# A piece held back at the chunk borders, the last sums on VectorE, and the first x copied earlier

## The chip, the cores and the metric

The kernel runs on one core of a Trainium2 chip. The core has five engines that run side by side, each through its own list of instructions: TensorE (PE in the profile, with its weight loads as PEld), VectorE (DVE), ScalarE (ACT), GpSimd (POOL) and SyncE (SP, which here only issues DMAs). The metric is the device time of one execution in microseconds (us), as the median of several runs.

## The reference

All arithmetic is float32. Attention comes first: 8 batches of 8 heads, 576 positions, 64 values a head, and in each row of scores only the 32 largest survive. The result is laid out as 4608 tokens of 512 values, and a two-layer MLP with an exact gelu follows.

```python
scores = scale * np.matmul(q, k.transpose(0, 1, 3, 2))          # (8, 8, 576, 576)
kth = np.partition(scores, -32, axis=-1)[..., -32:-31]
scores = np.where(scores >= kth, scores, -1e9)
attn = np.exp(scores - scores.max(-1, keepdims=True))
attn = attn / (attn.sum(-1, keepdims=True) + 1e-09)
x = np.matmul(attn, v).transpose(0, 2, 1, 3).reshape(4608, 512)
h = x @ w_in                                                    # 4608 x 2048
out = (0.5 * h * (1.0 + erf(h / sqrt(2)))) @ w_out              # 4608 x 512
```

## The kernel before

**Items and steps.** The attention is cut into 144 items. An item is a pair of heads and a tile of 128 queries (the last 64 queries of two pairs share an item). The main loop (L1034) makes one step `n` per item and works on several items at once. In step `n` TensorE makes the scores of items ahead (`scores`, L358; even steps make two), the product of item `n - 3` with v (`attend`, L596; only every second item has one, since two query tiles are multiplied together), and the transposes of the attention weights of item `n - 2` (`transposes`, L513). ScalarE evicts the scores, does the softmax of item `n - 1` in two halves (`softmax`, L490), copies transposed weights (L537, L560, L574) and copies the product into `xT` (L620). VectorE searches the 32nd largest score of item `n` (`top_k`, L423). GpSimd normalises the weights of item `n - 1` (`normalise`, L507), and in its list this stands behind two small operations that wait for the threshold VectorE has found (`threshold`, L470).

**Chunks and MLP pieces.** The MLP works on chunks of 256 tokens (one in five has 128). A chunk can begin when all four head pairs of its tokens have been multiplied with v. Its work is cut into pieces of a few matmuls, and the pieces stand in one fixed list, `pieces` (L956): blocks of the first layer (`l1_piece`, L664, matmuls on L673) alternate with blocks of the second layer of an earlier unit (L755, L773 and L776, or `products`, L792, with matmuls on L809 and L811). Most chunks use a scheme of seven products for a 2 by 2 block product, so that sums of the gelus are needed first (`sums`, L698, four additions on GpSimd, L704 to L707).

`mlp(n)` (L959) issues the next `n` pieces unless the next one needs tokens that are not there (`pieces[done[0]][0] > ready[0]`) or the step's allowance `left[0]` is used up. The loop calls it in many places, so that TensorE has MLP work between attention work. `room_in(n)` (L973) gives about one block per step, and the first-layer block of a new 256-token chunk begins in just the step that makes the last product of its tokens. Such a step is called a chunk border here; from step 18 on there are 15, all with even numbers.

**Around the border.** After the product the loop asks for `copy_x` and for a piece, but at a border the next piece needs the tokens that have only just been multiplied. L1062 catches this case: the eight transposes of the next item are issued directly behind the product (`turned`), then the tails' transposes, and `ready` is set to the new tokens.

```python
product = attend(n - 3)
...
copy_x()
...
mlp(1)
...
turned = tr.pop() if few[0] and tr else None
if product and n > START and done[0] < len(pieces) and pieces[done[0]][0] > ready[0]:
    if turned:
        turned()
```

**The ends.** `START` is 10: step 10 completes the first chunk. In the steps up to it a softmax half is issued on ScalarE (L1052) ahead of the copy of the product. Behind the last step, only MLP pieces are left; the last unit pair has the number `NU - 2`, and `last_parts` (L882) makes and stores the last 256 rows' sums on VectorE.

PSUM tiles are shared by tag. The transposes and half of the scores use `pr`; the first layer and the other half of the scores use `l1`; the product, the tails and the seventh product use `z`. Each has one buffer, so that a writer waits until the earlier content has been evicted.

Of the kernel before, what the change touches and what calls it, by code (L numbers as in the profile page):

```python
# [14 lines left out]
def kernel(  # L15
# [19 lines left out]
    nc = tc.nc  # L35
# [289 lines left out]
    def pair_tile(name, tag="pr"):  # L325
        return ps.tile([P, 2, 512], f32, tag=tag, bufs=1, name=name)
# [186 lines left out]
    def transposes(i):  # L513

        if i < 0 or i >= N:
            return []
        t, s = items[i][1], S_of.pop(i)
        pr = [None]

        def tails(ahead):  # L520
            tp = bank("tp_t")
            keys = last_keys(ahead, tp) if ahead is not None and ahead < N else None
            at = P
            if t % 2 == 0:
                pt_now[0] = work.tile([P, 2 * NM + 1, 2 * P], f32, tag="pt", bufs=1, name="pt")
            if t < NM:
                nc.tensor.transpose(tp[:, at : at + P], s[:, SM : S + TL], ident)  # L527
            else:
                for r in range(2):
                    nc.tensor.transpose(  # L530
                        tp[0:TL, at + r * P : at + (r + 1) * P],
                        s[:, r * S + SM : (r + 1) * S], ident,
                    )
            if keys:
                keys()
            if t < NM:
                nc.scalar.copy(  # L537
                    out=pt_now[0][:, 2 * NM, t % 2 * P : (t % 2 + 1) * P], in_=tp[:, at : at + P]
                )
                return  # L540
            for e in range(2):
                c = slice(e * TL, (e + 1) * TL)
                nc.scalar.copy(
                    out=halves(pt_end[c, 0, :], e, P),
                    in_=halves(tp[0:TL, at : at + 2 * P], e, P),
                )

        x = t % 2 * P if t < NM else 0

        def turn_over(tp, e):  # L550
            first = e * (S + TL if t < NM else S)
            for j in range(NM):
                nc.tensor.transpose(  # L553
                    tp[:, j * P : (j + 1) * P], s[:, first + j * P : first + (j + 1) * P], ident
                )

        def main(e):
            tp = bank("tp")
            turn_over(tp, e)
            nc.scalar.copy(  # L560
                out=pt_now[0][:, e * NM : (e + 1) * NM, x : x + P],
                in_=tp.rearrange("p (j n) -> p j n", j=NM),
            )

        def turn_both():
            pr[0] = tp = pair_tile("tp")
            for e in range(2):
                turn_over(tp[:, e], e)

        def both():  # L570
            if pr[0] is None:
                turn_both()
            tp = pr[0]
            nc.scalar.copy(  # L574
                out=pt_now[0][:, 0 : 2 * NM, x : x + P],
                in_=tp.rearrange("p e (j n) -> p (e j) n", j=NM),
            )

        if few[0]:
            return [tails, lambda _: both(), turn_both]  # L580
        return [tails] + [lambda _, e=e: main(e) for e in range(2)]

    def copy_x():
        while copies:
# [113 lines left out]
    def sums(u):  # L698

        g = g_of[u].rearrange("p x (f n) -> p x f n", f=2)  # L700
        a11, a21, a12, a22 = (g[:, :, f, h * P : (h + 1) * P] for f in range(2) for h in range(2))
        t = work.tile([P, 2, 3, P], f32, tag="sum", bufs=1, name="sum")
        s1, s2, s4 = (t[:, :, x] for x in range(3))
        nc.gpsimd.tensor_tensor(s1, a21, a22, op=ALU.add)  # L704
        nc.gpsimd.tensor_tensor(s2, s1, a11, op=ALU.subtract)
        nc.gpsimd.tensor_tensor(a21, a11, a21, op=ALU.subtract)
        nc.gpsimd.tensor_tensor(s4, a12, s2, op=ALU.subtract)  # L707
        sums_of[u] = t

    def weight_sums(j):  # L710
# [171 lines left out]
    def last_parts(tok, k, a):  # L882

        dve, add = nc.vector.tensor_tensor, ALU.add
        if k == 0:
            end_of["y"] = y0, y1 = y_tile(), y_tile()
            nc.scalar.copy(out=y0[:, B1], in_=a[:, 0])
            end_of["a"] = a
            return
        y0, y1 = end_of["y"]  # L890
        s7 = y7[0]
        if k == 1:
            dve(y0[:, B2], a[:, 0], y0[:, B1], op=add)
            dve(y0[:, B1], end_of["a"][:, 1], y0[:, B1], op=add)
            nc.sync.dma_start(out=out[last_row : last_row + P, B1], in_=y0[:, B1])
            dve(s7, s7, y0[:, B2], op=add)
            dve(y1[:, B2], a[:, 1], s7, op=add)
            nc.sync.dma_start(out=out[last_row + P : last_row + 2 * P, B2], in_=y1[:, B2])
            dve(y0[:, B2], a[:, 1], y0[:, B2], op=add)
            return  # L900
        dve(y0[:, B2], a[:, 1], y0[:, B2], op=add)
        nc.sync.dma_start(out=out[last_row : last_row + P, B2], in_=y0[:, B2])
        dve(y1[:, B1], s7, a[:, 0], op=ALU.subtract)
        nc.scalar.dma_start(out=out[last_row + P : last_row + 2 * P, B1], in_=y1[:, B1])
# [129 lines left out]
    for n in range(ahead):  # L1034

        left[0] = room_in(n)
        few[0] = n > START + 2
        eager[0] = n > N
        if not waits(unit_in(n)):
            weights_add(unit_in(n))  # L1040
        larger(n + 1)
        for piece in squares_in.pop(n, []):
            piece()
        two = few[0] and n % 2 == 0 and n + 3 < N and items[n + 3][1] < NM
        scores(n + 2, two)
        if two:
            scores(n + 3)
        product = attend(n - 3)
        late = n > START
        if n <= START:  # L1050

            softmax(n - 1, 0)  # L1052
        copy_x()
        if waits(unit_in(n)):
            weights_size(unit_in(n))
            weights_add(unit_in(n))
        mlp(1)
        if few[0] and n % 2:
            run_gelus()
        tr = transposes(n - 2)  # L1060
        turned = tr.pop() if few[0] and tr else None
        if product and n > START and done[0] < len(pieces) and pieces[done[0]][0] > ready[0]:  # L1062

            if turned:
                turned()
            for piece in tr[:1]:
                piece(n + 2 if few[0] else None)
            tr, ready[0] = tr[1:], n_tok[0]
        if not few[0] and n > START:
            softmax(n - 1, 0)  # L1070
        mlp(1)
        if not late:
            softmax(n - 1, 1)
        if few[0]:
            softmax(n - 1, 0)
            if n % 2:
                mlp(ODD)
        mlp(1)
        if n < START:

            keep_busy((4 if product or n == 0 else 14) * (1 if n < 5 else 2), ident)
        prep = prep_in.pop(n, [])
        if n == START + 1:

            for piece in prep:
                piece(None)
            prep = []
        if len(prep) > 1 and len(tr) == 3:
            tr, prep = tr[:1] + prep[:1] + tr[1:], prep[1:]
        now = tr[:-1]  # L1090
        if few[0]:
            now, tr, prep = tr + prep[:1], [], prep[1:]
        for x, piece in enumerate(now):
            piece(n + 2 if few[0] else None)
            if n < START and product and x == 0:
                keep_busy(5 if n < 5 else 10, ident)
            ready[0] = n_tok[0]
            if few[0] and x == 2:
                break
            mlp(1)  # L1100
        ready[0] = n_tok[0]
        if late:
            softmax(n - 1, 1)
        smaller(n + 1)
        add_small(n - 1)
        for piece in tr[-1:] + prep:
            piece(None)
            mlp(1)
        if n == 1:
            keep_busy(8, ident)  # L1110

        run_gelus()
        mlp(left[0])
        run_gelus()
        if n < N:
            top_k(n, lambda: inverse(n - 1))
        else:
# [54 lines left out]
```

## Time and profile before

| what | before |
|---|---|
| median of 3 runs | 1548.0 us (1547.71 to 1549.83) |
| the profiled execution | 1547.88 us |
| its span, first to last instruction | 1546.1 us |
| mean granted TensorE clock | 0.996 |
| TensorE busy | 1513.3 us, 98% |
| VectorE busy | 1336.4 us, 86% |
| ScalarE busy | 1160.4 us, 75% |
| GpSimd busy | 1142.8 us, 74% |
| TensorE, weight loads | 1193.3 us, 77% |

The profile is one execution, recorded by the hardware. An instruction's row has its start and its length in microseconds, its engine, its line in the kernel, its operation, the tile written and the tiles read, and, in brackets, how long the engine was idle before it and which instruction ended that idle time. Matmuls are pipelined and overlap, and their ends are modelled. In the list of waits a row reads: engine, what waited, what it waited for, the total, how many times, and the longest. A product of float32 matrices shows as two TensorE instructions for each matmul of the code, a transpose as one.

### The profile page before, as it was taken

The numbers are of one execution on the slowest core, as the hardware profiler recorded it, in microseconds if no ns is written. First come the engines' busy times: TensorE is split into PE (matmuls) and PEld (weight loads), VectorE is DVE, ScalarE is ACT, GpSimd is POOL, SyncE is SP. The second block draws the span as 40 slices with busy tenths as digits, with TensorE's granted clock in tenths as the row PEclk, the third lists the DMA queues.
The fourth block names the chain that finished last, engine by engine and source line by source line (L and its number), as shares of the span: only waits on it lengthen the run. The fifth ranks groups of instructions, "written<-read, shape, count | busy, mean of one in ns | idle before, by whom it ended". The sixth has DMA issues, their size and how long they took to land. (4 is left out here: it accounts for less than half of the span.)

```text
span 1546.1 us, 28114 instructions
## 1 busy us (share of the span) xinstructions
PE 1513.3 (98%) x9240; PEld 1193.3 (77%) x9240; DVE 1336.4 (86%) x4583; ACT 1160.4 (75%) x2038; POOL 1142.8 (74%) x1291
## 2 busy tenths in 40 slices
PE   7899999999999999999999999999999999999998
PEld 5676577877777777888777778788778777788887
DVE  8999999989989988899989998988998998888700
ACT  6999987777777777777777777777777777787720
POOL 4896657777787868767787877776788787877732
PEclk9999999999999999999999999999999999999999
DMA  6424310012101110012201111011110111000000
GB/s 161 149 99 113 86 46 1 18 35 39 24 15 31 38 35 19 1 30 46 40 14 20 27 32 45 1 25 36 32 24 22 24 30 32 15 1 15 8 14 14
DMA packets 195027, 56.36 MB, mean 36 GB/s; under 512 B 185888, under 2 KB 186432, under 8 KB 194880
## 3 DMA queue, kind: packets, MB, share of 16 engines
q1 hardware_dynamic: 193616, 54.14, 14.9%
q8 instruction: 73, 1.20, 0.3%
q14 instruction: 74, 0.61, 0.1%
q10 hardware_dynamic: 1200, 0.39, 0.1%
q0 software_dynamic: 64, 0.03, 0.0%
HBM read 45.08 MB, written 9.44 MB: 35 GB/s over the span
## 5 line engine op out<-in xcount | busy, mean ns | idle before, releaser
L673 PE MATMUL h_ps<-xT,w_in_sb 128*128 128x256 f32 (+1 forms) x2560 | 539.6, 361 | 1.8 <-ACT xT L620 1.7
L673 PEld LDWEIGHTS h_ps<-xT,w_in_sb 128*128 128x128 f32 x2560 | 434.9, 191 | 73.5 <-issue 25.3
L450 DVE MAX8 top<-lists 128x8 f32<-128x288 f32 x792 | 321.4, 448 | 0.0
L507 POOL TENSOR_TENSOR s<-s,rden 128x1152 f32<-128x1152 f32 x144 | 302.9, 2104 | 0.3 <-DVE rden L482 0.3
L496 ACT ACTIVATE s<-s,bias 128x576 f32<-128x576 f32 x288 | 223.3, 775 | 11.9
L453 DVE MATCH_REPLACE8 lists<-top,lists 128x288 f32<-128x288 f32 x528 | 229.9, 443 | 0.0
L495 ACT ACTIVATE s<-s,neg 128x576 f32<-128x576 f32 x288 | 225.7, 784 | 2.9 <-POOL neg L475 2.8
L450 DVE MAX8 low<-lists 128x8 f32<-128x288 f32 x528 | 213.2, 446 | 0.0
L574 ACT COPY pt<-tp 128x1024 f32<-128x1024 f32 x133 | 134.9, 1014 | 95.9 <-PE tp L553 95.9
L488 POOL TENSOR_SCALAR den<-den 128x2 f32<-128x2 f32 x144 | 31.6, 219 | 224.6 <-ACT s L496 220.9
L421 POOL TENSOR_TENSOR lists<-lists 128x576 int32<-128x576 int32 x132 | 186.3, 1412 | 4.0
L413 POOL TENSOR_TENSOR lists<-s 128x576 int32<-128x576 int32 x132 | 185.9, 1408 | 0.0
L553 PE MATMUL tp<-ident,s 128*128 128x128 f32 x1152 | 150.4, 273 | 8.2 <-POOL s L507 8.2
L553 PEld LDWEIGHTS tp<-ident,s 128*128 128x128 f32 x1152 | 133.5, 141 | 27.9 <-POOL s L507 14.5
L615 PE MATMUL o<-pt,raw_v 128*64 128x256 f32 x1280 | 153.7, 385 | 0.4 <-ACT pt L560 0.4
L615 PEld LDWEIGHTS o<-pt,raw_v 128*64 128x64 f32 x1280 | 87.3, 137 | 86.1 <-issue 45.7
L475 POOL TENSOR_SCALAR neg<-kth 128x2 f32<-128x2 f32 x132 | 85.9, 651 | 90.6 <-DVE kth L466 90.0
L811 PE MATMUL y_ps<-w_out_sb,sum 128*128 128x256 f32 x480 | 142.8, 379 | 0.0
L378 ACT ACTIVATE s<-s_ps 128x1024 f32<-128x1024 f32 x127 | 124.2, 1025 | 15.1 <-PE s_ps L370 15.0
L370 PE MATMUL s_ps<-kt,qm 64*128 64x512 f32 x512 | 131.2, 626 | 0.8 <-ACT s L376 0.8
L482 DVE RECIPROCAL rden<-den 128x2 f32<-128x2 f32 x144 | 23.4, 162 | 124.0 <-POOL den L488 122.3
L453 DVE MATCH_REPLACE8 lists<-low,lists 128x288 f32<-128x288 f32 x264 | 115.0, 444 | 0.0
(148 smaller groups left out, 2771.3 us busy)
## 6 DMA issues: line engine op xcount, KB each, us to landing
raw_v<-in_v_dram SPq DMA_DIRECT2D x64, 128.0 KB, 2.3
out_dram<-y SPq DMA_DIRECT2D x30, 256.0 KB, 2.1
raw_q<-in_q_dram SPq DMA_DIRECT2D x112, 64.0 KB, 2.0
raw_k<-in_k_dram SPq DMA_DIRECT2D x112, 64.0 KB, 2.0
w_out_sb<-in_moe_w_in_dram SPq DMA_DIRECT2D x14, 511.8 KB, 4.7
w_out_sb<-in_moe_w_out_dram SPq DMA_DIRECT2D x10, 511.8 KB, 4.3
w_sum<-in_moe_w_out_dram SPq DMA_DIRECT2D x6, 511.8 KB, 4.2
raw_q<-in_q_dram SPq DMA_DIRECT2D x112, 8.0 KB, 1.8
```

The source lines that it names most:

```text
L413: nc.gpsimd.tensor_tensor(t[:, 1].bitcast(i32), a.bitcast(i32), b.bitcast(i32), op=ALU.add)
L421: nc.gpsimd.tensor_tensor(both, both, top, op=ALU.subtract)
L450: nc.vector.max(x[:, e], src[:, e])
L453: nc.vector.match_replace(dst[:, e], x[:, e], src[:, e], LOWEST)
L495: nc.scalar.activation(s, s, func=AF.Prelu, bias=st["neg"][:, e : e + 1], scale=1.0, alpha=STEEP)
L496: nc.scalar.activation(s, s, func=AF.Exp, bias=st["bias"][:, e : e + 1], scale=1.0, accum_out=st["den"][:, e : e + 1],)
L507: nc.gpsimd.tensor_tensor(s, s, wide, op=ALU.mult)
L553: nc.tensor.transpose(tp[:, j * P : (j + 1) * P], s[:, first + j * P : first + (j + 1) * P], ident)
L574: nc.scalar.copy(out=pt_now[0][:, 0 : 2 * NM, x : x + P], in_=tp.rearrange("p e (j n) -> p (e j) n", j=NM),)
L615: nc.tensor.matmul(o[e * D : (e + 1) * D, 0:n], lhsT=vt[:, j, e, :], rhs=pt[:, e * NM + j if j < NM else 2 * NM, :], start=(j == 0), stop= ...
L673: nc.tensor.matmul(h_tile(u)[:, i, :], lhsT=w_in_sb[:, ko, f * P : (f + 1) * P], rhs=xT[:, ko, c0 : c0 + n], start=(ko == 0), stop=(ko == ...
L811: nc.tensor.matmul(acc[names][:, k], lhsT=lhsT, rhs=rhs, start=(j == 0 and k == 0), stop=(j == FT // 2 - 1 and k == 1),)
```

## The change

- **Borders.** A new function `closes(i)` tells whether item `i`'s product completes a 256-token chunk. In the step before a border the allowance is one piece smaller, in the border step one larger. So the `mlp(1)` behind `copy_x` has a piece of an older chunk to issue right after the product, and then `ready` is set to the new tokens. The following `mlp(1)` calls find first-layer pieces, and the transposes come at the place that they have in all other steps. The special path with `turned` is gone.
- **Last sums.** For the unit pair `NU - 2` the four sums of the gelus are made by VectorE, into a buffer of the `s` tiles, which the attention no longer uses by then, and not into the single `sum` buffer.
- **Last store.** In `last_parts` the addition for one quarter of the output, and its store, are made with the first pair of products (`k == 0`), in a tile of its own, and not with the second.
- **First chunk.** In step 10 the first softmax half is issued behind `copy_x`.

```diff
+    def closes(i):
+        if not few[0] or i < 0 or i >= N:
+            return False
+        pair, t = items[i]
+        return t < NM and t % 2 == 1 and pair % NP == NP - 1
...
-        t = work.tile([P, 2, 3, P], f32, tag="sum", bufs=1, name="sum")
+        if u == NU - 2:
+            t = work.tile([P, 2 * S], f32, tag="s", bufs=6, name="sum_s")
+            t = t[:, 0 : 6 * P].rearrange("p (x k n) -> p x k n", x=2, k=3)
+            add = nc.vector.tensor_tensor
+        else:
+            t = work.tile([P, 2, 3, P], f32, tag="sum", bufs=1, name="sum")
+            add = nc.gpsimd.tensor_tensor
         s1, s2, s4 = (t[:, :, x] for x in range(3))
-        nc.gpsimd.tensor_tensor(s1, a21, a22, op=ALU.add)
...
+        add(s1, a21, a22, op=ALU.add)
+        add(s2, s1, a11, op=ALU.subtract)
+        add(a21, a11, a21, op=ALU.subtract)
+        add(s4, a12, s2, op=ALU.subtract)
...
         if k == 0:
             end_of["y"] = y0, y1 = y_tile(), y_tile()
             nc.scalar.copy(out=y0[:, B1], in_=a[:, 0])
-            end_of["a"] = a
+            first = part_tile()
+            dve(first, a[:, 1], y0[:, B1], op=add)
+            nc.sync.dma_start(out=out[last_row : last_row + P, B1], in_=first)
             return
...
             dve(y0[:, B2], a[:, 0], y0[:, B1], op=add)
-            dve(y0[:, B1], end_of["a"][:, 1], y0[:, B1], op=add)
-            nc.sync.dma_start(out=out[last_row : last_row + P, B1], in_=y0[:, B1])
...
         eager[0] = n > N
+        left[0] += closes(n - 3) - closes(n - 2)
...
-        if n <= START:
+        if n < START:
             softmax(n - 1, 0)
         copy_x()
+        if n == START:
+            softmax(n - 1, 0)
...
         mlp(1)
+        if closes(n - 3):
+            ready[0] = n_tok[0]
         if few[0] and n % 2:
             run_gelus()
         tr = transposes(n - 2)
-        turned = tr.pop() if few[0] and tr else None
         if product and n > START and done[0] < len(pieces) and pieces[done[0]][0] > ready[0]:
-            if turned:
-                turned()
```

More of the change, by code (lines that the diff above doesn't have):

```diff
@@ L517, in transposes @@
         t, s = items[i][1], S_of.pop(i)
-        pr = [None]
         def tails(ahead):
@@ L563, in main, with both @@
             )
-        def turn_both():
-            pr[0] = tp = pair_tile("tp")
+        def both():
+            tp = pair_tile("tp")
             for e in range(2):
                 turn_over(tp[:, e], e)
[L570 to L573, printed above, removed]
             nc.scalar.copy(
@@ L579, in transposes @@
         if few[0]:
-            return [tails, lambda _: both(), turn_both]
+            return [tails, lambda _: both()]
         return [tails] + [lambda _, e=e: main(e) for e in range(2)]
+    def closes(i):
[3 more added lines that the diff above has]
+        return t < NM and t % 2 == 1 and pair % NP == NP - 1
     def copy_x():
@@ L701, in sums @@
         a11, a21, a12, a22 = (g[:, :, f, h * P : (h + 1) * P] for f in range(2) for h in range(2))
-        t = work.tile([P, 2, 3, P], f32, tag="sum", bufs=1, name="sum")
+        if u == NU - 2:
[5 more added lines that the diff above has]
+            add = nc.gpsimd.tensor_tensor
         s1, s2, s4 = (t[:, :, x] for x in range(3))
[L704 to L707, printed above, removed]
+        add(s1, a21, a22, op=ALU.add)
+        add(s2, s1, a11, op=ALU.subtract)
+        add(a21, a11, a21, op=ALU.subtract)
+        add(s4, a12, s2, op=ALU.subtract)
         sums_of[u] = t
```

## The prediction

> **What bounds the kernel now.** I read the page's busy times first, then the waits of TensorE, then the timeline around those waits.
>
> ```profile
> span 1546.1 us, 28114 instructions
> ## 1 busy us (share of the span) xinstructions
> PE 1513.3 (98%) x9240; PEld 1193.3 (77%) x9240; DVE 1336.4 (86%) x4583; ACT 1160.4 (75%) x2038; POOL 1142.8 (74%) x1291
> ```
>
> TensorE is idle for 32.8 us in all (1546.1 less 1513.3). The list of its waits says where (total, times, longest):
>
> ```profile
> PE tp L553 <- POOL s L507: 8.2, 13, 1.1
> ...
> PE seven L809 <- POOL g L706: 2.4, 1, 2.4
> PE h_ps L673 <- ACT xT L620: 1.7, 1, 1.7
> ```
>
> The rows left out lie in the opening, before the MLP has begun. These three add up to 12.3 us, and the parts of the change touch these three places. The thirteen waits of the first row are at the chunk borders; the other two come once each, at the last block and at the first chunk. The price of a piece comes from the chain of waits, where the six products pieces of a block are one row:
>
> ```profile
> 1528.17 5.19 PE y_ps L811 x24
> ```
>
> Six pieces in 5.19 us are 0.86 us a piece. Now one border with a wait, the odd step behind it, and the border that has none:
>
> ```profile
> 388.75 1.99 PE L370 MATMUL s_ps<-kt,qm 64*128 64x512 f32 x8
> 390.66 2.38 PE L615 MATMUL o<-pt,raw_v 128*64 128x256 f32 x20
> 393.54 1.09 PE L553 MATMUL tp<-ident,s 128*128 128x128 f32 x8 [0.50 <-POOL s L507]
> ...
> 405.39 0.27 PE L527 MATMUL tp_t<-ident,s 128*128 128x128 f32 x1
> ...
> 1405.59 2.38 PE L615 MATMUL o<-pt,raw_v 128*64 128x256 f32 x20
> 1407.90 1.09 PE L553 MATMUL tp<-ident,s 128*128 128x128 f32 x8
> ```
>
> From the start of the product to the start of the transposes it takes 2.88 us with a wait of 0.50 us and 2.31 us without: a wait costs about 0.07 us more than its bracket says.
>
> **Part 1, the borders.** Held back is the last piece of the step before (0.86 us, no longer there), and it is issued right after the product (0.86 us, new there): no TensorE work is added. What moves is the order. Scores and product of the border step begin 0.86 us earlier; behind the product come the held piece, two first-layer pieces, and only then the transposes, where before the transposes came directly.
>
> The transposes need the weights that GpSimd normalises at L507. Measured from the modelled end E of the product as it is now, they are ready 0.3 to 1.1 us after E. In the new order the product ends at E - 0.86, and three pieces (2.6 us) follow: the first transpose is due about 1.6 us after E, later than the longest wait. So all thirteen waits should go: 8.2 + 13 x 0.07 = 9.1 us. The border at 1407.90 has nothing to lose or win, and the last border, in the steps after the softmaxes, has no wait either.
>
> What could be late next? First, the copy of x. Here are the rows of ScalarE at the same border:
>
> ```profile
> 387.12 1.01 ACT L574 COPY pt<-tp 128x1024 f32<-128x1024 f32 x1 [0.51 <-PE tp L553]
> ...
> 389.92 1.94 ACT L378 ACTIVATE s<-s_ps 128x1024 f32<-128x1024 f32 x2 [0.21 <-PE s_ps L370]
> 393.12 0.37 ACT L620 COPY xT<-o 128x256 f32<-128x256 f32 x1 [1.25 <-PE o L615]
> ```
>
> The copy starts 0.08 us after the product's end and takes 0.37 us, so it ends near E - 0.4. A first-layer piece reads two of the four row blocks of x, and only the fourth is written by this copy. It is needed in the middle of the second first-layer piece, about 1.1 us after E: a margin of 1.5 us. Second, the scores. The second pair of scores shares its PSUM tile with the transposes of the step before, which the copy at 387.12 empties at 388.13. Those scores start half way through the 1.99 us, at 389.7, and 0.86 us earlier is 388.85: 0.7 us of margin. ScalarE itself could begin the eviction 0.21 us sooner and then ends at 391.65, before the product's new end (392.2). Third, the softmax half that was issued behind the tails' copies now comes ahead of them; the tails' PSUM bank is asked for again only in the next step. SP's and GpSimd's queues hold no moved DMA here.
>
> Bounds of this part: nothing gained (the waits move) and 9.1 us. It could come out below nothing only if x came late, which is a rival below. I take 9.1 since each margin above is larger than what it has to cover.
>
> Does TensorE keep what it wins? It does if the others can follow. DVE's waits over the run, and in the 80 us between two borders:
>
> ```profile
> DVE rden L482 <- POOL den L488: 122.3, 91, 8.1
> ```
> ```profile
>   POOL den L488: 7.0, 6
> ```
>
> DVE waits 7.0 us between 394 and 474 us, and a border wins 0.4 to 1.2 us. In the step behind a border the normalised weights stand ready well before use (this row ends at 403.56, and the transpose above starts at 405.39):
>
> ```profile
> 401.46 2.10 POOL L507 TENSOR_TENSOR s<-s,rden 128x1152 f32<-128x1152 f32 x1
> ```
>
> That is 1.8 us of margin against 0.6 us won at that border. So GpSimd and DVE should follow.
>
> [...]
>
> **Part 2, the sums of the last gelus.** The four sums of the last block leave GpSimd for DVE, into a tile of their own.
>
> ```profile
> 1535.79 1.13 PE L809 MATMUL seven<-w_sum,g 128*128 128x256 f32 x4 [2.43 <-POOL g L706]
> ```
> ```profile
> 1533.53 0.72 POOL L704 TENSOR_TENSOR sum<-g 128x256 f32<-128x256 f32 x1 [9.37 <-PE y_ps L811]
> ```
> ```profile
> 1527.43 1.09 ACT L689 ACTIVATE g<-h_ps 128x512 f32<-128x512 f32 x2 [11.60 <-PE h_ps L673]
> ```
> ```profile
> 1541.02 0.42 DVE L894 TENSOR_TENSOR y<-y_ps,y 128x256 f32<-128x256 f32 x1
> 1541.36 0.41 DVE L896 TENSOR_TENSOR y<-y,y 128x256 f32<-128x256 f32 x1
> ```
>
> The gelus end at 1528.52, but GpSimd waited until 1533.53 for the products that still read the single sum tile. With another tile DVE can start at 1528.5, and it has nothing else to do. Four additions of the form of L896 (0.41 us) end near 1530.2, three microseconds before TensorE wants them. The wait of 2.43 us goes, and with it the restart of some 0.1 us: 2.5 us, bounded by 0 and 2.6. GpSimd's next small addition no longer queues behind the sums.
>
> **Part 3, the last store.** One DVE addition (L894) leaves the closing chain; it is made earlier, while DVE is idle, and its DMA on SP's queue is issued earlier too, by itself. L894 to L896 start 0.34 us apart, and those rows follow each other without a wait, so the end moves by 0.34 us at most. I take 0.3 (bounds 0 and 0.34).
>
> **Part 4, the first chunk's x.**
>
> ```profile
> 103.89 2.73 PE L615 MATMUL o<-pt,raw_v 128*64 128x256 f32 x20
> ...
> 108.39 0.60 PE L673 MATMUL h_ps<-xT,w_in_sb 128*128 128x256 f32 x2
> 110.70 0.70 PE L673 MATMUL h_ps<-xT,w_in_sb 128*128 128x256 f32 x2 [1.72 <-ACT xT L620]
> ...
> 117.47 0.27 PE L527 MATMUL tp_t<-ident,s 128*128 128x128 f32 x1
> ```
> ```profile
> 108.68 0.76 ACT L495 ACTIVATE s<-s,neg 128x576 f32<-128x576 f32 x1
> ...
> 110.30 0.35 ACT L620 COPY xT<-o 128x256 f32<-128x256 f32 x1
> ```
> ```profile
> 113.90 2.10 POOL L507 TENSOR_TENSOR s<-s,rden 128x1152 f32<-128x1152 f32 x1
> ```
>
> The product ended at 106.62, so a copy placed ahead of the softmax half starts at 108.68 instead of 110.30, and TensorE goes on 1.62 us sooner. ScalarE's work in this step is only reordered; the softmax half starts about 0.3 us later, and the second half, behind both, keeps its time. What is late next is the normalising at 113.90, which ends at 116.00 whatever TensorE does: the transpose of 117.47 can come at most 1.41 us sooner. I take 1.4, with bounds 0 and 1.6.
>
> **The sum.** 9.1 + 2.5 + 0.3 + 1.4 = 13.3 us. The profiled execution took 1547.88 us (its span 1546.1 and 1.8 around it), 0.12 us under the median of 1548.0. 1547.9 - 13.3 = 1534.6, and against the median 1534.7; I forecast 1534.6, 0.87% faster.
>
> **Rivals.** *A, part of the border gain comes back as new waits.* TensorE gets ahead, and GpSimd's normalising is late for other transposes. For it: L507 stands behind a wait for DVE, and a row of 1.8 us margin is one of many steps. Against it: DVE's 7.0 us of waits per 80 us. If half of 9.1 us returns, the time is 1539.2.
>
> *B, DVE sets the pace, or the held piece doesn't come to stand where it is meant to.* Then the border part wins nothing and the rest stays: 1547.9 - 4.2 = 1543.7. For it: DVE's 86%. Against it: 122.3 us of DVE's waits are for a value that TensorE's order of work releases.
>
> *C, slower: x arrives too late at the borders.* The transposes that covered the copy are gone from there; if ScalarE is busy when the product ends, the second first-layer piece stalls. The copy has 1.5 us to spare; each microsecond beyond that costs 15 us over 15 borders. At 2.4 us late the whole gain of 13.3 us is gone, and at 3 us late the time is 1547.9 - 13.3 + 22.5 = 1557. For it: at the first chunk the copy did stand 1.62 us behind a softmax half. Against it: ScalarE was waiting 1.25 us for the product in the row above, and no softmax is queued ahead of that copy.
>
> **How the numbers follow.** Main case 0.62, A 0.18, B 0.14, C 0.06. A difference of about 0.2% (3.1 us) is what a measurement of this kernel can tell from none. The main case alone spans 1532.5 to 1537 (the border part between 7 and 10, the first chunk between 1 and 1.6, the last block 2 to 2.6). The range also takes in A and reaches towards B: 1531 to 1541.5. Faster by over 0.2% (under 1544.9): main, A and most of B, 0.89. Within 0.2%: 0.05, the rest of B. Slower: 0.06, which is C.
>
> **What the profile of the changed kernel would show.** Part 1: no TensorE wait of a transpose for the normalised weights at a border, and pieces between product and transposes; waits of first-layer matmuls for x would be C, and waits for L507 in other steps A. If TensorE's waits are gone and the span is not, B. Part 2: four additions on DVE right after the last gelus and no wait of L809. Part 3: six DVE additions in the closing chain instead of seven. Part 4: the wait of the first chunk near 0.1 us, and perhaps a new one of 0.2 us at the next transposes. I would be wrong above all if the normalised weights move with TensorE's order and not with DVE's.

## The result, and the profile after

| what | before | after |
|---|---|---|
| median, runs taken together | 1548.91 us (6 runs, 1547.71 to 1549.86) | 1537.2 us (6 runs, 1536.61 to 1538.06) |
| ratio, 95% interval | | 0.9925 (0.9913 to 0.9938) |
| the profiled execution | 1547.88 us | 1538.06 us |
| its span | 1546.1 us | 1536.3 us |
| its granted TensorE clock | 0.996 | 0.994 |

The change makes the kernel 0.75% faster, by 11.7 us between the medians; 13.3 us were forecast. The forecast of 1534.6 is missed by 2.6 us: 1.6 are the gain's, and 1.0 comes from the base, since it was reckoned from a profiled execution of 1547.88 us and the median of before is 1548.91 in these runs. First the busy times of the changed kernel's page, then all of TensorE's waits behind step 10 from its list of waits (engine, what waited and for what, total, times, longest).

```profile
PE 1516.2 (99%) x9240; PEld 1195.8 (78%) x9240; DVE 1338.1 (87%) x4587; ACT 1159.7 (75%) x2038; POOL 1138.8 (74%) x1287
```
```profile
PE tp_t L526 <- POOL s L507: 1.7, 7, 0.3
...
PE o L616 <- ACT pt L559: 0.4, 1, 0.4
PE o L616 <- ACT pt L568: 0.2, 1, 0.2
```

The three rows that the prediction was after, 12.3 us together, are gone from the list: the waits of `tp` at the borders, of `seven` at the last block and of `h_ps` at the first chunk. TensorE is idle for 1536.3 - 1516.2 = 20.1 us, where it was 32.8. Some small rows have grown in their place, and they matter below.

To see where the time went, take the start of the same product with v in both traces, place by place. The last column is the lead of the changed kernel.

| place | before, us | after, us | after less before |
|---|---|---|---|
| product of step 10 (first chunk complete) | 103.89 | 105.88 | +1.99 |
| next product, step 12 | 120.69 | 121.24 | +0.55 |
| last product but one | 1461.55 | 1454.53 | -7.02 |
| `seven` of the last block | 1535.79 | 1526.48 | -9.31 |
| last addition on VectorE | 1543.01 | 1533.19 | -9.82 |

The first row is no effect of the change. All of its parts begin at that product or later, and the opening takes more or less time from one execution to the next: the same file run again reached this place at 104.21 us, and the time went with it (below). The granted clock goes with it as well: up to this product it was 0.92 in this profile and 0.95 in the one of before, and TensorE was busy for 92.2 us and not 89.2. That is the whole rise of its busy time, from 1513.3 to 1516.2 us. Without the opening the profile gained 9.8 + 2.0 = 11.8 us. The 11.7 us of the medians are closer to this than single executions are to each other: the six of before lie in two groups, 1547.7 to 1548.0 and 1549.8 to 1549.9, and those of the changed kernel between 1536.6 and 1538.1. By stage: 1.4 us at the first chunk, 7.6 us at the borders up to the last product but one, 0.3 us lost at the last border, 2.6 us up to the start of `seven` at the last sums, and 0.5 us behind it. Some 0.3 us of a long stretch is scatter: the traces of three runs below that change only the last sums or the first chunk are 0.3 us ahead of before between step 12 and the last product but one.

**A border.** TensorE's timeline at the border that the prediction quotes (start, length, engine, line, operation, written from read, count):

```profile
388.97 2.38 PE L616 MATMUL o<-pt,raw_v 128*64 128x256 f32 x20
391.28 0.70 PE L818 MATMUL y_ps<-w_sum,g 128*128 128x256 f32 x2
391.82 0.59 PE L818 MATMUL y_ps<-w_out_sb,sum 128*128 128x256 f32 x2
392.25 1.89 PE L674 MATMUL h_ps<-xT,w_in_sb 128*128 128x256 f32 x8
393.98 0.38 PE L333 MATMUL tp_t<-kt,qm 128*128 128x128 f32 x2
394.20 0.27 PE L526 MATMUL tp_t<-ident,s 128*128 128x128 f32 x1
394.31 1.03 PE L674 MATMUL h_ps<-xT,w_in_sb 128*128 128x256 f32 x4
395.17 1.04 PE L552 MATMUL tp<-ident,s 128*128 128x128 f32 x8
```

The order is the one described: product, held piece (L818), two first-layer pieces (L674), tails, a third first-layer piece, transposes (L552). The tails' transpose (L526) is the first instruction that needs the normalised weights. No row has a bracket: nothing waits for the weights, and the first-layer matmuls don't wait for x. But the first two matmuls of the held piece last 0.70 us, and the next pair starts 0.54 us after them, where pairs elsewhere follow each other at 0.43 us. So 0.11 us are still lost behind the product, as if it were a little of the restart that was to go with the wait.

**The new waits.** Three times, four steps behind a border that had waited 1.1 us before, a tail's transpose waits for the normalised weights. First TensorE's row, then the timeline of GpSimd ahead of it:

```profile
513.50 0.33 PE L526 MATMUL tp_t<-ident,s 128*128 128x128 f32 x1 [0.27 <-POOL s L507]
```
```profile
507.58 0.73 POOL L883 TENSOR_TENSOR y<-y,part 128x256 f32<-128x256 f32 x1
...
510.57 0.66 POOL L475 TENSOR_SCALAR neg<-kth 128x2 f32<-128x2 f32 x1 [0.59 <-DVE kth L466]
...
511.35 2.10 POOL L507 TENSOR_TENSOR s<-s,rden 128x1152 f32<-128x1152 f32 x1
```

GpSimd has no bracket here apart from 0.59 us in each step: in the two steps before it did the four sums of the gelus and eight small additions of the MLP. TensorE has gained on it, so that L507 ends 0.27 us late. Each of these waits takes 0.34 us of the lead.

**The last border.** Here the held piece does harm. One row:

```profile
1471.40 2.38 PE L616 MATMUL o<-pt,raw_v 128*64 128x256 f32 x20 [0.24 <-ACT pt L568]
```

The product is multiplied with transposed weights that ScalarE copies at L568. In the kernel before, the piece stood ahead of the product (it began at 1478.98 without a wait) and covered the copy. Held back, it no longer does. The held piece alone (below) brings the same wait of 0.24 us, and the traces that hold nothing back there don't have it.

**The first chunk.** The copy of x, the product, and the normalising that was to be late next, each from its engine's timeline:

```profile
110.58 0.36 ACT L621 COPY xT<-o 128x256 f32<-128x256 f32 x1
110.83 0.78 ACT L495 ACTIVATE s<-s,neg 128x576 f32<-128x576 f32 x1
```
```profile
115.80 2.10 POOL L507 TENSOR_TENSOR s<-s,rden 128x1152 f32<-128x1152 f32 x1
```
```profile
117.95 0.33 PE L526 MATMUL tp_t<-ident,s 128*128 128x128 f32 x1
```

Take the 1.99 us of the opening off: the copy starts at 108.59 (108.68 was said), the normalising at 113.81 (113.90), and the transpose follows 0.05 us behind its end. It is the limit that the prediction named.

**The last sums.** VectorE's timeline, and the rows of GpSimd and TensorE that go with it:

```profile
1521.84 0.43 DVE L711 TENSOR_TENSOR sum_s<-g 128x256 f32<-128x256 f32 x1 [57.16 <-ACT g L690]
1522.30 0.86 DVE L712 TENSOR_TENSOR sum_s<-sum_s,g 128x256 f32<-128x256 f32 x1
1523.08 0.41 DVE L713 TENSOR_TENSOR g<-g 128x256 f32<-128x256 f32 x1
1523.41 0.41 DVE L714 TENSOR_TENSOR sum_s<-g,sum_s 128x256 f32<-128x256 f32 x1
```
```profile
1522.15 0.72 POOL L839 TENSOR_TENSOR y<-y,p 128x256 f32<-128x256 f32 x1 [4.71 <-ACT p L837]
```
```profile
1526.48 1.03 PE L816 MATMUL seven<-w_sum,g 128*128 128x256 f32 x4
```

The sums are done at 1523.8, 2.7 us before `seven` wants them, and `seven` has no bracket.

### The profile page after: what moved, and what is told of

Same layout as the page of the kernel before. It is cut to its first block, busy times and chain, and to the rows that moved or that the text cites. A ratio compares the mean times of both kernels' runs of the same rounds, so it can differ in the third digit from the quotient of the medians.

```text
span 1536.3 us, 28097 instructions
## 1 busy us (share of the span) xinstructions
PE 1516.2 (99%) x9240; PEld 1195.8 (78%) x9240; DVE 1338.1 (87%) x4587; ACT 1159.7 (75%) x2038; POOL 1138.8 (74%) x1287
## 4 chain that ended last, share of the span: by engine, by line
PE 75%; POOL 11%; DVE 5%; ACT 1%; issue 1%; DVEq 0%; POOLq 0%
PE h_ps L674 27%; PE y_ps L818 15%; PE o L616 8%; PE tp L552 6%; PE s_ps L370 6%; POOL s L507 3%; PE seven L816 2%; PE y_ps L762 2%; PE y_ps L780 2%; PE y_ps L783 2%; POOL lists L413 1%; POOL lists L421 1%; DVE lists L453 1%; PE tp_t L333 1%; PE o L627 1%; DVE top L450 1%
## 5 line engine op out<-in xcount | busy, mean ns | idle before, releaser
L674 PE MATMUL h_ps<-xT,w_in_sb 128*128 128x256 f32 (+1 forms) x2560 | 544.2, 361 | 0.1
L674 PEld LDWEIGHTS h_ps<-xT,w_in_sb 128*128 128x128 f32 x2560 | 434.0, 191 | 71.1 <-issue 25.2
L507 POOL TENSOR_TENSOR s<-s,rden 128x1152 f32<-128x1152 f32 x144 | 302.7, 2102 | 0.3 <-DVE rden L482 0.3
L568 ACT COPY pt<-tp 128x1024 f32<-128x1024 f32 x133 | 135.1, 1016 | 112.3 <-PE tp L552 112.3
L552 PE MATMUL tp<-ident,s 128*128 128x128 f32 x1152 | 149.6, 273 | 0.0
L552 PEld LDWEIGHTS tp<-ident,s 128*128 128x128 f32 x1152 | 134.6, 141 | 14.7 <-issue 1.9
L818 PE MATMUL y_ps<-w_out_sb,sum 128*128 128x256 f32 x472 | 140.4, 379 | 0.0
```

The source lines that it names most:

```text
L507: nc.gpsimd.tensor_tensor(s, s, wide, op=ALU.mult)
L552: nc.tensor.transpose(tp[:, j * P : (j + 1) * P], s[:, first + j * P : first + (j + 1) * P], ident)
L674: nc.tensor.matmul(h_tile(u)[:, i, :], lhsT=w_in_sb[:, ko, f * P : (f + 1) * P], rhs=xT[:, ko, c0 : c0 + n], start=(ko == 0), stop=(ko == ...
L818: nc.tensor.matmul(acc[names][:, k], lhsT=lhsT, rhs=rhs, start=(j == 0 and k == 0), stop=(j == FT // 2 - 1 and k == 1),)
```

## The experiments

The theory was the prediction's: the borders gain because the transposes no longer stand where the weights are late. Against it stood that the borders win nothing (VectorE sets the pace), and that more comes back as new waits. Further runs split the parts; only the last store has no run of its own.

### The border part alone

```diff
+        left[0] += closes(n - 3) - closes(n - 2)
...
         mlp(1)
+        if closes(n - 3):
+            ready[0] = n_tok[0]
...
-        turned = tr.pop() if few[0] and tr else None
```

> The kernel before with the border part alone (held piece and new order); sums, last store and first copy as before. Both theories (the new order wins; the held piece wins) expect the same here: no wait of L552 for the normalised weights at a border, 8.5 us won at the thirteen border steps, 1.0 us lost again at three later steps (near 515, 878 and 1241 us), 0.3 us at the last border: 7.2 us under the kernel before. If the parts lean on each other, the sum of the parts measured alone differs from the 11.8 us that stand between the two traces.

Measured: 1543.08 us against 1548.13, ratio 0.9965 (0.9952 to 0.9977). From the product of step 10 (105.31 here) to `seven` of the last block, the last border included, the trace gains 7.0 us, with the same waits of tails' transposes as the changed kernel, 0.3 us at the longest: the border part is worth that much without the others. Yet the span fell by only 3.9 us. The opening took 1.4 of the rest, and the end 1.7: from the start of `seven` to the end of the span it took 12.0 us here and 10.3 before. Two stretches of the end, in the view by windows (us in the stretch, busy time of each engine with its instructions, granted clock, DMA share, GB/s), show why:

```profile
1527.31:1530.73 3.42, 0.99 (x6) 0.54 (x5) 0.00 (x0) 0.00 (x0) 2.73 (x4) 1.00 0.00 0
1530.73:1534.14 3.41, 3.41 (x10) 2.70 (x9) 0.00 (x0) 0.37 (x1) 1.49 (x3) 0.50 0.00 0
```

TensorE waits 2.43 us for GpSimd's last sums in the first stretch, and in the next its granted clock is 0.50: ten instructions in 3.41 us, where the same view shows sixteen in 3.00 us at full pace. This wait is in the kernel before too, without that drop. The section on the hardware takes it up.

### The held piece alone, the old order kept

```diff
+        left[0] += closes(n - 3) - closes(n - 2)
```

> The kernel before with the held piece alone: one piece fewer in the step before a border, one right after the product, and then the transposes at once, as before. Theory order: product and held piece together end when the product ended before, so the transposes wait for the same normalised weights: 13 waits, 8 us in all, and no time won (0 to 0.3 us lost). Theory hold: the piece covers 0.86 us of the wait, so at most the 1.1 us waits remain in part: 7 us won.

Measured: 1550.08 us against 1548.13, ratio 1.0007 (0.9998 to 1.0016): no gain. In the trace 0.3 us are lost from the product of step 10 to `seven` of the last block, all of it at the last border. The waits at the borders stay, a little shorter, in the list of waits and at the border of 390 us:

```profile
PE tp L553 <- POOL s L507: 5.4, 11, 0.9
```
```profile
390.20 2.38 PE L622 MATMUL o<-pt,raw_v 128*64 128x256 f32 x20
392.51 0.70 PE L818 MATMUL y_ps<-w_sum,g 128*128 128x256 f32 x2
393.05 0.59 PE L818 MATMUL y_ps<-w_out_sb,sum 128*128 128x256 f32 x2
393.94 1.09 PE L553 MATMUL tp<-ident,s 128*128 128x128 f32 x8 [0.30 <-POOL s L507]
```

The piece stands between product and transposes, 0.86 us of cover against a wait of 0.50, and a wait of 0.30 us is left. The product comes 0.86 us sooner, so the cover begins sooner by as much; the transposes still start when the weights come. A piece that is only moved across the product covers nothing.

### The order alone, nothing held back

```diff
         copy_x()
...
+        if closes(n - 3):
+            ready[0] = n_tok[0]
         mlp(1)
...
-        turned = tr.pop() if few[0] and tr else None
```

> The kernel before with the new order alone: nothing is held back; at a border the first-layer pieces of the new chunk follow the product directly, and the transposes come after them. Theory order: the first two row blocks of x are long there, the fourth is needed 1.2 us after the product's modelled end and its copy lands 0.5 us after it, so there is no wait for x, and the thirteen waits go: 7.5 us won, 0.3 more than with the held piece, since the last border keeps its cover of the copy of the transposed weights. Theory hold: without the held piece TensorE waits for x at every border, 0.5 us and more, and nearly nothing is won.

Measured: 1543.89 us against 1548.13, ratio 0.9964 (0.9950 to 0.9978). First-layer pieces now follow the product at once. The border's row, and the waits of the tails' transposes:

```profile
391.70 2.86 PE L674 MATMUL h_ps<-xT,w_in_sb 128*128 128x256 f32 x12
```
```profile
PE tp_t L526 <- POOL s L507: 1.9, 7, 0.4
```

Twelve matmuls run in one row without a wait for x, though the copy has nothing but the first of them to hide behind. From the product of step 12 to the last but one the trace gains 5.8 us; the part with the held piece gains 7.3 us on the same way, of which the last border takes 0.3 back. At the borders themselves both win the same; in the steps behind them this one loses 0.9 us three times, where the other loses 0.34. So the order brings the gain, and the held piece adds some 1.2 us to it.

### The changed kernel without the held piece

```diff
-        left[0] += closes(n - 3) - closes(n - 2)
...
-        mlp(1)
         if closes(n - 3):
             ready[0] = n_tok[0]
+        mlp(1)
```

> The changed kernel without the held piece, with its order and its three other parts. Theory order: as the changed kernel, or 0.3 us faster, 12 us under the kernel before. Theory hold: 7 us slower than the changed kernel.

Measured: 1538.30 us against 1548.13, ratio 0.9933 (0.9920 to 0.9947). Corrected for the opening (0.5 us here) its profile is 10.6 us ahead of before, the changed kernel's 11.8. The difference of 1.2 us is the one of the run above, now with the other parts in place. The medians cannot tell it from nothing: the intervals overlap. Why GpSimd normalises some 0.4 us later at these places when nothing is held back is not settled.

### The last sums, split into tile and engine

GpSimd keeps the sums, in a tile of their own:

```diff
+        if u == NU - 2:
+            t = work.tile([P, 2 * S], f32, tag="s", bufs=6, name="sum_s")
```

> The kernel before with one change: the last block's four sums stay on GpSimd but get a tile of their own. Theory tile (the wait was for the products that still read the single sum tile): GpSimd starts at the end of the gelus, 1528.5 on the clock of the trace before, and its four sums of 2.9 us end before TensorE is through with the block ahead at 1533.2; the wait of L809 is gone, 2.6 us won without DVE. Theory engine (GpSimd is too slow): part of the wait stays.

Measured: 1545.29 us against 1549.96, ratio 0.9975 (0.9965 to 0.9984). VectorE makes them, in the one tile that all blocks share:

```diff
+        add = nc.vector.tensor_tensor if u == NU - 2 else nc.gpsimd.tensor_tensor
```

> The kernel before with the last block's four sums on DVE, in the single sum tile that they shared before. Theory tile: DVE too waits for the last product that reads the tile, and only the shorter additions are won: the third of them ends after some 1.3 us and not 2.2, so TensorE waits about 1.4 to 1.5 us and not 2.43; 1.0 us won. Theory engine: the wait goes.

Measured: 1547.30 us against 1549.96, ratio 0.9984 (0.9975 to 0.9993). The first sum on GpSimd with its own tile and `seven` behind it, and then the same two rows with VectorE's sums in the shared tile:

```profile
1528.71 0.72 POOL L708 TENSOR_TENSOR sum_s<-g 128x256 f32<-128x256 f32 x1 [4.43 <-ACT g L689]
```
```profile
1533.31 1.03 PE L813 MATMUL seven<-w_sum,g 128*128 128x256 f32 x4
```
```profile
1533.95 0.42 DVE L705 TENSOR_TENSOR sum<-g 128x256 f32<-128x256 f32 x1 [61.80 <-PE y_ps L812]
```
```profile
1535.31 0.89 PE L810 MATMUL seven<-w_sum,g 128*128 128x256 f32 x3 [1.50 <-DVE g L707]
```

With the own tile GpSimd starts as soon as the gelus are there (its bracket names ScalarE's gelu), and the wait is gone altogether: from the `seven` of the block ahead to the last one it takes 2.59 us less than before. With the shared tile VectorE must wait for the products that read it (its bracket names TensorE), and 1.50 of 2.43 us remain; 0.93 us are won. The tile alone takes the whole wait away, the engine alone only a part. The medians differ by more, 4.7 and 2.7 us. The 26 executions of before in these rounds lie between 1547.5 and 1551.2 us, and what the longer ones spent the time on was not profiled.

### The first chunk's x alone

```diff
-        if n <= START:
+        if n < START:
             softmax(n - 1, 0)
         copy_x()
+        if n == START:
+            softmax(n - 1, 0)
```

> The kernel before with the first chunk's copy alone ahead of the softmax half. The wait of 1.7 us falls to 0.1, the next transposes meet the normalised weights, 1.4 us won at the product of step 12 and kept to the end (no border changes). At the end the wait of 2.43 us for the last sums stands; in the three profiles so far that end with this wait and began later, the granted clock fell to half for 3.4 us there, in the profile of before it didn't: where it falls the end takes 1.7 us more.

Measured: 1548.20 us against 1549.96, ratio 0.9988 (0.9978 to 0.9997). The lead at the product of step 12 is 1.39 us, and all of it is kept to the last block; 1.8 us lie between the medians. The half clock that was thought possible came (0.50 from 1535.34 to 1538.75 us): from the start of `seven` the end took 12.0 us, where it took 10.3 before.

### Fewer small additions in a step

The new waits of 0.27 us were put down to GpSimd's small additions. Here a step makes fewer of them, and the last border holds nothing back.

```diff
-        if not few[0] or i < 0 or i >= N:
+        if not few[0] or i < 0 or i >= N - 1:
...
-        run_small(6)
+        run_small(5)
```

> The changed kernel with two small edits: at most five small additions per step on GpSimd (six before), and nothing held back for the very last border. Theory: the wait of 0.27 us that is new three times (at 513.5, 876.4 and 1239.4) comes from GpSimd, which adds up a chunk's output for two steps without a pause and comes late to the normalising; one addition fewer per step makes room, and 0.3 us come back each time. At the last border 0.3 us come back as well, 1.3 us in all under the changed kernel. Rival: these waits are set by DVE's search, and only the 0.3 us of the last border come back.

Measured: 1543.33 us against 1549.96, ratio 0.9960 (0.9947 to 0.9973): slower than the change with its 0.9925. The waits in question did go, and so did that of the last border, but three others came, 1.5 to 2.7 us long:

```profile
545.56 0.33 PE L526 MATMUL tp_t<-ident,s 128*128 128x128 f32 x1 [2.59 <-POOL s L507]
```

SP's queue, here and then in the changed kernel (start, time to the end of the last of the row's transfers, line, written from read, count), and VectorE's waits here:

```profile
515.93 7.55 SPq L741 DMA_DIRECT2D out_dram<-y  x2
523.58 5.12 SPq L109 DMA_DIRECT2D raw_k<-in_k_dram  x8
```
```profile
507.66 1.05 SPq L741 DMA_DIRECT2D out_dram<-y  x2
521.39 4.02 SPq L109 DMA_DIRECT2D raw_k<-in_k_dram  x8
```
```profile
530.03 0.85 DVE L268 STREAM_TRANSPOSE kt<-raw_k 128x640 f32<-128x640 f32 x1 [1.51 <-DMA raw_k<-in_k_dram]
534.08 0.31 DVE L270 STREAM_TRANSPOSE kt<-raw_q 128x128 f32<-128x128 f32 x1 [3.20 <-DMA raw_q<-in_q_dram]
```

The store of a finished block waits on SP for its last small addition, which now comes a step later. The loads of the next heads' k and q are queued behind that store, and k starts 2.2 us later (523.58 and 521.39), although this execution is 1.8 us ahead of the other there (product of the next step at 526.92 and 528.75). VectorE waits for them, 1.51 and 3.20 us, GpSimd waits 5.23 us for VectorE's threshold ahead of the normalising, and TensorE waits 2.59 us. A transfer that nobody waits for had been in front of one that everybody needs.

### The stores issued one step later

On top of the run above, a finished block's store is kept back until the end of the next step.

```diff
+    held = []
+
+    def later(tok, y):
+        if eager[0]:
+            store(tok, y)
+        else:
+            held.append((tok, y))
+
+    def flush():
+        while held:
+            store(*held.pop(0))
...
-            store(tok + P, y1)
+            later(tok + P, y1)
...
-            store(tok, y0)
+            later(tok, y0)
...
-        run_small(6)
+        flush()
+        run_small(5)
```

> The run with five small additions per step, and in addition the stores of a chunk's last two tiles are issued one step later, behind the loads that SP issues in that step. Theory: the waits of 1.5 to 2.7 us that came up there (near 545, 911 and 1276 us) come from SP, where two stores that wait for GpSimd's later additions stand ahead of the loads of q and k; with the stores behind the loads they go, and the winnings of that run remain: 0.34 us three times where the wait of 0.27 us was, 0.6 us three times some 100 us later, 0.3 us at the last border, 3 us in all under the changed kernel. Rival: the additions themselves come too late on GpSimd, and the waits near 545, 911 and 1276 us stay.

Measured: 1534.15 us (4 runs, 1532.38 to 1535.69) against 1549.74 before, ratio 0.9899 (0.9885 to 0.9912). Run beside it, the changed kernel took 1536.47. The row of tails' transposes in its list of waits is down to the one in the opening:

```profile
PE tp_t L526 <- POOL s L507: 0.3, 1, 0.3
```

With stores out of the loads' way, the fewer additions do what they were meant to: up to the last product but one this version is 3.1 us ahead of the changed kernel, counted from the product of step 10: three times 0.34 us at the new waits, three times 0.6 us some 100 us later, where the kernel before waited already, and 0.3 us at the second border. Behind 122 us no wait of TensorE above 0.06 us is left in the trace. It is faster than both kernels, than the changed one by 2.3 us between the medians.

### The changed kernel again

Nothing edited.

> The changed kernel as it is, on the same chip as the run before it. Both theories: 0.7 to 0.8% under the kernel before. Its opening is that of the kernel before, so that a spread of 1 to 2 us between executions, if it comes from the clock granted in the opening, shows here too, while the drop of the clock at the last sums cannot.

Measured: 1536.47 us against 1549.74, ratio 0.9918 (0.9904 to 0.9931), with the product of step 10 at 104.21 us and a span of 1534.7 us. Its steps at the borders are the same to 0.02 us. The 2 us of the first profile's opening are thus the execution's and not the change's. Between the medians lie 13.3 us here and 11.7 in the first runs; the two traces, each without its opening, say 11.7 and 11.8. That 13.3 was also the forecast says nothing for the forecast.

## Why the prediction was right or wrong

**What bounds the kernel.** Right: time fell by what TensorE no longer waited, and it did not go to VectorE, which is 87% busy after. Had VectorE set the pace, the border part would have won nothing and rival B's 1543.7 us would have been left; the border part alone gained 7.0 us in its trace.

**Part 1, 9.1 us: the mechanism right, the size 1.9 us too large.** All thirteen waits went. Three terms make the difference.

*"13 x 0.07", the restart:* the thirteen borders gained 8.5 us, not 9.1, which is 0.02 us each beyond the wait. The 0.07 us came from one border with a wait and one without. The prediction took it that this loss goes with the wait, but the held piece behind the product loses 0.11 us of its own, as its row of 0.70 us shows, where the transposes that stood there lost 0.05 (1.09 us for eight, and 1.04 in their new place).

*"GpSimd and DVE should follow":* VectorE did. GpSimd did not at three places, four steps behind a border, where many small additions had piled up, and 3 x 0.34 = 1.0 us came back. That is rival A in small. The margin of 1.8 us had been read at one step. At these three places the trace of before leaves less than 0.1 us, as in these rows of GpSimd and TensorE:

```profile
513.44 2.11 POOL L507 TENSOR_TENSOR s<-s,rden 128x1152 f32<-128x1152 f32 x1
```
```profile
515.63 0.33 PE L527 MATMUL tp_t<-ident,s 128*128 128x128 f32 x1
```

The run with fewer additions bears out the source, since these three waits went with them. At other places before left no margin at all. The prediction says that the rows of waits it leaves out lie in the opening, but this one does not:

```profile
PE tp_t L527 <- POOL s L507: 0.8, 4, 0.3
```

The longest of the four, 0.29 us, lies in the step of the first chunk, and the other three, 0.18 us each, near 609, 974 and 1339 us. They were a sign for rival A, and the changed kernel still has them among its seven.

*"The last border ... has no wait either":* true before, but the held piece had covered a copy on ScalarE there. 0.3 us were lost.

So 8.5 - 1.0 - 0.3 = 7.2 us; the small shifts beside them come to less than 0.1 us. The dangers named were rightly dismissed: x was never late (rival C), even with first-layer pieces right behind the product. What the prediction could not say is which half matters. It counted three pieces between product and transposes as cover; the runs show that the first-layer pieces are the cover, and the held piece by itself brings nothing. With the new order it is worth some 1.2 us, for a reason that stays open.

**Part 2, 2.5 us: 2.7 measured**, 2.6 up to the start of `seven` and 0.1 behind it, since `seven` at full pace takes 1.03 us and behind the wait it took 1.13. The cause was as given: the tile, and not the engine. Not foreseen was the half clock behind the same wait: in the border part alone it was 0.50 for 3.41 us, and the end took 12.0 us from the start of `seven`, 1.7 more than the 10.3 in the profile of before. Whether it came in other executions of before, no profile shows.

**Part 3, 0.3 us: 0.4 measured**, the 0.5 us behind the start of `seven` less the 0.1 just named. The runs with the last sums alone end 10.2 us after the start of `seven`, and the changed kernel 9.8. The bound of 0.34 was too tight: the additions take 0.26 us less from the first start to the last, and the first starts 0.15 us sooner behind `seven`, which the sum did not have. No run made this edit alone.

**Part 4, 1.4 us: 1.4 measured**, twice, and with the limit named.

**The sum.** 7.2 + 2.7 + 0.4 + 1.4 = 11.7 us against 13.3; the 1.6 us that are missing are those of part 1, less the 0.3 that parts 2 and 3 gave more.

## What to carry to other kernels

Before work is put in front of a wait, ask whether its start moves along with what it is to cover: here a piece taken from before the product and put behind it won nothing (ratio 1.0007), while work put there that was to come after the wait won 5.8 us in the trace (ratio 0.9964). Where TensorE gains, look up the tightest margin of its suppliers over all steps, not the margin of one; and look what a DMA queue holds behind a store before the store is made to wait longer; here it was the loads of k, which started 2.2 us later. The wait of 2.43 us on a single shared buffer was settled by a second buffer alone, on either engine.

## What the runs showed of the hardware

**One wait, two prices.** The same wait of 2.43 us for the last sums was followed by half the clock in the border part alone, the held piece alone, the order alone and the x copy alone, and not in the profile of before. In the order alone this shows as a clock of 0.71 between 1530 and 1533 us and 0.72 between 1533 and 1536, in the other three as 0.50 over 3.41 us. In the profile of before the granted clock is 0.50 from 19.05 to 22.47 us and from 46.36 to 53.19 us, 23.89 us apart: one, two and seven stretches of 3.41 us. In that of the changed kernel it changes at 18.15, 24.97, 38.63, 42.04, 48.87 and 55.69 us, again whole stretches of this length apart. Counted on in such stretches, the wait lies differently in them from one trace to the other. Here are two at the wait in the kernel before, then two in the one with only x copied earlier, from the view by windows:

```profile
1531.16:1534.57 3.41, 2.19 (x11) 1.58 (x9) 0.00 (x0) 0.00 (x0) 0.96 (x2) 1.00 0.00 0
1534.57:1537.99 3.42, 2.20 (x10) 1.97 (x11) 0.00 (x0) 0.37 (x1) 2.94 (x5) 1.00 0.02 5
```
```profile
1531.93:1535.34 3.41, 0.98 (x5) 0.60 (x4) 0.00 (x0) 0.00 (x0) 2.83 (x5) 1.00 0.00 0
1535.34:1538.75 3.41, 3.41 (x10) 2.69 (x9) 0.00 (x0) 0.37 (x1) 1.38 (x2) 0.50 0.02 5
```

Before, the wait is split, 1.22 us in one stretch and 1.21 in the next, TensorE is busy for 2.19 us of each, and the clock stays. In the other all of it falls into one stretch, 0.98 us of work are left there, and the next stretch has half the clock. The three waits of the run with fewer additions lie on both sides in one trace:

```profile
543.43:546.85 3.42, 1.29 (x8) 1.14 (x9) 3.42 (x13) 3.14 (x6) 3.42 (x3) 1.00 0.28 46
546.85:550.26 3.41, 3.41 (x14) 2.57 (x13) 3.41 (x13) 1.94 (x3) 1.44 (x2) 0.50 0.29 48
...
1273.88:1277.30 3.42, 1.72 (x12) 1.57 (x13) 3.42 (x14) 2.70 (x6) 3.34 (x3) 1.00 0.00 0
1277.30:1280.71 3.41, 3.41 (x20) 1.73 (x19) 3.41 (x14) 3.00 (x5) 1.30 (x2) 1.00 0.00 0
```

A busy time of 1.29 us in a stretch is followed by half the clock, 1.72 us is not, although this second wait is longer (2.73 us, split in two). By idle time, in the stretches read behind the openings: 2.13 us (the first above), 2.14 (the held piece alone) and 2.43 (the border part alone and the x copy alone) were followed by a clock of 0.50; 1.22 (before, at the last sums), 1.50 (the shared tile), 1.52 and 1.70 (the other two waits of the run with fewer additions) and 1.72 (before, at the first chunk, 107.80 to 111.22 us) were followed by 1.00. Idle time alone does not separate them in the openings: in the changed kernel's a stretch with 1.57 us idle, 35.21 to 38.63 us, was followed by 0.50 too. What brings the drop is not shown beyond that.

The six times of before lie in two groups, 1547.7 to 1548.0 and 1549.8 to 1549.9. The 1.8 us between the groups are close to the 1.7 us by which the border part's end was longer; that the second group had the drop is an estimate from these two numbers, as no such run was profiled. A longer time at half clock in the opening, as in the first profile of the changed kernel (17.1 us at 0.50, and 10.2 in the one of before), would fit as well.

**Two engines on one addition.** On VectorE L712 took 0.86 us while GpSimd ran L839, and its neighbours of the same shape 0.41 to 0.43 us; in the run with the shared tile, with no GpSimd row beside them, all four took 0.42 us. Why the addition takes twice as long beside GpSimd's is not shown: no run varied it by itself.
